# Banded attention and two mixer blocks in one kernel: a weight's split halves issued ahead of the exponentials, early row scaling on one engine, two masks built on GpSimd

## The chip, the core and the metric

The kernel runs on one core of a Trainium2 chip. The metric is the device time of one launch in microseconds (us), the median of several runs; less is better. Five engines run their own instruction queues in order and wait for one another by semaphores: TensorE (PE; the loading of its weights is listed as PEld), VectorE (DVE), ScalarE (ACT), GpSimd (POOL) and SyncE (SP), which here only starts transfers.

## The reference, cut to what matters

```
attention, batch 2, 8 heads, 768 positions, head size 64:
  s = (q @ k^T) / 8
  keep = (key < n_sink) | (0 <= query - key < window)      # n_sink 4, window 128
  a = softmax(where(keep, s, -1e9));  x = a @ v            # [2, 768, 512]
mixer 1:  h = relu(x @ w_in);  u, v = halves of h
          v_n = layernorm(v);  gated = u * (w_spatial @ v_n + b);  x = gated @ w_out
mixer 2:  u = x + token MLP(x);  out = u + channel MLP(u)
```

All matrices of the mixers are multiplied as high and low halves: a product takes three matmuls, high by high, low by high, high by low. So every weight must be split into a high part (a rounding copy) and a low part (the weight less its high part) before it is used. The weights `w_in` and others arrive as 64-bit floats, whose words VectorE first shifts and merges into 32-bit floats.

## The kernel before, in words

**Stages.** The attention comes first; the first matrix of mixer 1 (`w_in`) is worked beside it, in pieces called fills, since TensorE has time to spare there. The rest of the mixers follows and depends on TensorE nearly alone.

**Steps of the attention.** A block is 128 queries (12 blocks `j`: 6 for each of 2 batches); a step `n` (from -3 on, 24 of them with all parts) is half a block, 4 heads. The loop of `banded` (L339) is a software pipeline written out by hand: in step `n` it issues, in this order, the reciprocal of the row sums of step n+1 (`sums`, DVE L184 and L185), the transposes of step n's weights (PE L253) and their copies out of PSUM (`a_out`: ACT L261; and for a block that has a left neighbour DVE `aL`, L264), the scaling of step n+1 (`norm`), the score matmuls of step n+3 (PE L177), their masking and row maximum (`scores`: DVE L202 and L207), the exponentials of step n+2 (`expo`: ACT L223, 4 of them), and in even steps the difference of two blocks of v (`v_step`: POOL `dv`, L271). Then come the preparation of a weight (`pump`), the product with v of step n-1 (PE `pv`, L287), every second step the result of a block (`x_out`: ACT `xTH` L315, DVE `xTL` L316) and fills. Each engine's queue has its instructions in the order of issue; nothing reorders them.

**The product with v has one accumulator.** `pv` of a new block can only start when `xTL` of the block before has been read out of it (DVE L316).

**Weights.** In steps -1 to 6 (`PUMPS`) one 128x512 piece of `w_in` is prepared in each: three DVE instructions merge the words into `wi` (L464, L468, L471). Its halves are issued by `flush` one step later, from `pump`: the high part on ACT (L482) and the low part on POOL (L483). The last one has a `flush` of its own in step 7 (L366).

**Scaling.** `norm` multiplies the 4 heads' exponentials by their reciprocals: heads 0 and 1 by an ACT instruction each (L238), heads 2 and 3 by one POOL instruction (L234); the few sink columns of all 4 by another POOL instruction (`eS`, L242).

**Masks.** `masks` (L89) builds three masks on DVE before the first `scores`. m0 is needed first (step -3 and -2), m1 in step -1, m2 from step 1 on.

Of the kernel before, what the change touches and what calls it, by code (L numbers as in the profile page):

```python
# [12 lines left out]
ALU = mybir.AluOpType  # L13
PSUM = bass.MemoryType.PSUM

P = 128
# [8 lines left out]
SK = 16  # L25
# [4 lines left out]

LQ, LE, LN = 3, 2, 1
PUMPS = range(-1, 7)
BUDGET = 1900


# [4 lines left out]
class Kernel:  # L40
# [48 lines left out]
    def masks(self, pool):  # L89
        nc = self.nc  # L90
        V = nc.vector
        ta, tb = (pool.tile([P, 4, P], F32, name=x, tag=x, bufs=2) for x in ("aT", "aL"))
        rel, pos, kD, kP, kS, t = *(ta[:, x] for x in range(4)), tb[:, 0], tb[:, 1]
        nc.gpsimd.iota(rel, pattern=[[-1, P]], base=0, channel_multiplier=1, allow_small_or_imprecise_dtypes=True)
        nc.gpsimd.iota(pos, pattern=[[1, P]], base=0, channel_multiplier=0, allow_small_or_imprecise_dtypes=True)

        self.low = pool.tile([P, P], F32, name="low")
        self.up = pool.tile([P, P], F32, name="up")
        self.lowT = pool.tile([P, P], F32, name="lowT")
        V.tensor_scalar(out=self.low, in0=rel, scalar1=0.0, scalar2=None, op0=ALU.is_ge)  # L100
        V.tensor_scalar(out=self.up, in0=rel, scalar1=0.0, scalar2=None, op0=ALU.is_lt)
        V.tensor_scalar(out=self.lowT, in0=rel, scalar1=0.0, scalar2=None, op0=ALU.is_le)
        self.scalars(self.cp)
        m0 = pool.tile([P, P], F32, name="m0")
        m1 = pool.tile([P, KW], F32, name="m1")
        m2 = pool.tile([P, KW], F32, name="m2")

        def put(dst, keep):
            V.tensor_scalar(out=dst, in0=keep, scalar1=NEG, scalar2=-NEG, op0=ALU.mult, op1=ALU.add)

        V.tensor_scalar(out=kD, in0=rel, scalar1=self.win, scalar2=None, op0=ALU.is_lt)
        V.scalar_tensor_tensor(out=kD, in0=rel, scalar=0.0, in1=kD, op0=ALU.is_ge, op1=ALU.mult)
        V.tensor_scalar(out=kS, in0=pos, scalar1=self.ns, scalar2=None, op0=ALU.is_lt)

        V.tensor_tensor(out=t, in0=kD, in1=kS, op=ALU.max)
        put(m0, t)

        V.tensor_scalar(out=kP, in0=rel, scalar1=float(P), scalar2=self.win, op0=ALU.add, op1=ALU.is_lt)
        V.tensor_tensor(out=t, in0=kD, in1=kP, op=ALU.max)
        put(m1[:, 0:P], t)  # L120
        put(m2[:, 0:P], t)
        put(m2[:, P:KW], kS[:, 0:SK])

        V.tensor_tensor(out=t[:, 0:SK], in0=kS[:, 0:SK], in1=kP[:, 0:SK], op=ALU.is_gt)
        put(m1[:, P:KW], t[:, 0:SK])
        self.msk = [m0, m1, m2, m2, m2, m2]

# [100 lines left out]
    def norm(self, g):  # L228

        nc = self.nc  # L230
        j, ph = divmod(g, 2)
        r = self.rs[g]
        e = self.e[j][:, 4 * ph : 4 * ph + 4]
        nc.gpsimd.tensor_tensor(  # L234
            out=e[:, 2:4, 0:P], in0=e[:, 2:4, 0:P], in1=r[:, 2:4].unsqueeze(2).to_broadcast([P, 2, P]), op=ALU.mult
        )
        for c in range(2):
            nc.scalar.activation(out=e[:, c, 0:P], in_=e[:, c, 0:P], func=AF.Copy, scale=r[:, c : c + 1])  # L238
        if j % NB:
            if ph == 0:  # L240
                self.eS[j] = self.ap.tile([P, H, SK], F32, name="eS", tag="eS", bufs=2)
            nc.gpsimd.tensor_tensor(  # L242
                out=self.eS[j][:, 4 * ph : 4 * ph + 4], in0=e[:, :, P:KW],
                in1=r.unsqueeze(2).to_broadcast([P, 4, SK]), op=ALU.mult,
            )
# [79 lines left out]
    def banded(self):  # L325
        self.q, self.vb, self.vsb, self.ps_s, self.ss, self.e, self.sm, self.rs = {}, {}, {}, {}, {}, {}, {}, {}
        self.aT, self.ps_x, self.aS, self.dv, self.eS = {}, {}, {}, {}, {}
        NJ = B * NB
        self.kr = self.ap.tile([P, NC4, RING, KW], F32, name="kr")
        self.vf = self.ap, "vf", 2  # L330
        self.scalar_loads(self.cp)
        self.load_qk(0, 2)
        self.warm(10)
        self.load_qk(1)
        self.prefetch()
        self.load_v(0)
        self.load_qk(2)
        self.masks(self.ap)
        for n in range(-LQ, NG + 2):  # L339
            j, ph = divmod(n, 2)  # L340
            self.xdone = self.xnext
            if ph and n >= -1:
                if (n + 7) // 2 < NJ:
                    self.load_qk((n + 7) // 2)
                if (n + 3) // 2 < NJ:
                    self.load_v((n + 3) // 2)
            if 0 <= n + LN < NG:
                self.sums(n + LN)
            if 0 <= n < NG:
                self.a_transpose(n)  # L350
                self.a_out(n)
            if 0 <= n + LN < NG:
                self.norm(n + LN)
            if n + LQ < NG:
                self.qk(n + LQ)
                if n < 0:
                    self.warm(3)
                self.scores(n + LQ)
            if 0 <= n + LE < NG:
                self.expo(n + LE)  # L360
            if 0 <= n < NG and ph == 0 and j % NB:
                self.v_step(j)
            self.step()
            if n in PUMPS:
                self.pump()
            if n == max(PUMPS) + 1:  # L366
                self.flush()
            if 0 <= n - 1 < NG:
                self.pv(n - 1)
                if ph == 0:  # L370
                    if (j - 1) % NB:
                        self.sinks_mm(j - 1)

                    self.fill_until(j - 1)
                    self.x_out(j - 1)
            if 0 <= n < NG and ph == 1 and j % NB:
                self.sinks(j)
            if n == NG - 4:
                self.raws = [self.spatial_load(r) for r in range(2)]
            self.fill(BUDGET)  # L380
        self.xdone = self.xnext
        self.vf = self.sp, "tmp", 4
# [541 lines left out]
```

## Time and profile before

| | |
|---|---|
| median of 3 runs | 499.09 us (498.95 to 500.24) |
| the profiled execution | 499.52 us, its span 497.7 us |
| busy: PE, DVE, ACT, POOL | 95%, 56%, 35%, 29% of the span |
| mean granted TensorE clock | 0.978 of 2.4 GHz |
| PE in 40 slices | `8589799999999999999999899999999999999994` |
| DVE in 40 slices | `6989864675553489946979798765222211311112` |
| granted clock in 40 slices | `9859899999999999999999999999999999999998` |

One slice is 12.4 us. A digit is the busy share in tenths, or the granted clock in tenths. The share of the whole span says little here: the first five slices are another program than the rest, as the digits of PE and DVE show. Everything that the change touches runs in the first 75 us.

### The profile page before, as it was taken

What the parts mean: (1) busy time and instruction counts of PE and PEld (TensorE: products, weight loads), DVE (VectorE), ACT (ScalarE), POOL (GpSimd) and SP (SyncE); (2) the same over time, 40 slices, a digit from 0 to 9 for tenths busy, and PEclk for the clock granted to TensorE, in tenths of its full rate; (3) what the DMA queues carried; (4) which work ended last, traced back from release to release, by engine and by line L of the source; (5) the groups of instructions that cost most, each with busy time, mean ns of one, the idle gap of its engine ahead of it and who ended that gap; (6) DMA issues with size and microseconds to landing.
All of it is one profiled execution on the core that took longest, in us unless ns stands there. A gap on an engine that the chain in (4) does not pass through costs nothing.

```text
span 497.7 us, 7141 instructions
## 1 busy us (share of the span) xinstructions
PE 473.5 (95%) x2672; PEld 395.4 (79%) x2672; DVE 280.5 (56%) x631; ACT 176.5 (35%) x471; POOL 145.3 (29%) x164
## 2 busy tenths in 40 slices
PE   8589799999999999999999899999999999999994
PEld 7357588788888999998888578888888888888883
DVE  6989864675553489946979798765222211311112
ACT  4556677686754322235542222222101110011000
POOL 1453742354344557652543133222100000000000
PEclk9859899999999999999999999999999999999998
DMA  8844131402005022313544244221020000200002
GB/s 265 264 149 139 65 97 38 153 23 86 2 2 211 1 84 65 96 32 105 170 127 131 83 126 128 84 86 42 2 84 0 1 0 1 85 1 0 0 1 91
DMA packets 19788, 38.82 MB, mean 78 GB/s; under 512 B 1825, under 2 KB 8225, under 8 KB 19745
## 3 DMA queue, kind: packets, MB, share of 16 engines
q1 hardware_dynamic: 19312, 38.02, 24.1%
q8 instruction: 23, 0.38, 0.3%
q10 hardware_dynamic: 432, 0.26, 0.2%
q14 instruction: 21, 0.16, 0.1%
HBM read 35.13 MB, written 3.15 MB: 77 GB/s over the span
## 4 chain that ended last, share of the span: by engine, by line
PE 82%; DVE 13%; ACT 1%; issue 1%; DMA 1%; POOL 0%; POOLq 0%; ACTq 0%
PE pso L59 7%; PE pso L57 7%; PE pso L58 7%; PE psc L57 6%; PE psc L59 6%; PE psc L58 6%; PE pv L287 4%; PE psg L59 3%; PE psg L58 3%; PE psg L57 3%; PE sc L177 3%; DVE wi L468 2%; PE psu L57 2%; PE ps L59 2%; PE ps L57 2%; PE ps L58 2%
## 5 line engine op out<-in xcount | busy, mean ns | idle before, releaser
L630 DVE SCALAR_TENSOR_TENSOR hh<-psc,hh 128x512 fp32r<-128x512 f32 x36 | 24.9, 692 | 127.9 <-ACT hh L629 127.8
L629 ACT ACTIVATE hh<-psc 128x512 fp32r<-128x512 f32 x36 | 21.5, 597 | 157.1 <-PE psc L59 157.1
L59 PE MATMUL pso<-c2H,hh 128*128 128x512 f32 x144 | 56.3, 391 | 1.2 <-DVE hh L630 1.2
L57 PE MATMUL pso<-c2H,hh 128*128 128x512 f32 x144 | 56.8, 394 | 0.0
L58 PE MATMUL pso<-c2L,hh 128*128 128x512 f32 x144 | 56.1, 390 | 0.0
L471 DVE SCALAR_TENSOR_TENSOR wi<-rawi,wi 128x512 int32<-128x512 int32 (+2 forms) x46 | 41.2, 895 | 1.6
L223 ACT ACTIVATE e<-s,nm 128x144 f32<-128x144 f32 (+1 forms) x96 | 38.1, 399 | 4.0 <-DVE nm L207 4.0
L468 DVE SCALAR_TENSOR_TENSOR wi<-rawi,wi 128x512 int32<-128x512 int32 (+2 forms) x46 | 36.4, 791 | 1.6
L464 DVE TENSOR_SCALAR wi<-rawi 128x512 int32<-128x512 int32 (+2 forms) x46 | 32.8, 712 | 0.7 <-POOL c1L L483 0.6
L59 PEld LDWEIGHTS pso<-c2H,hh 128*128 128x128 f32 x144 | 27.0, 188 | 7.3 <-DVE hh L630 1.6
L57 PE MATMUL psg<-wsTH,vnH 128*128 128x384 f32 x96 | 32.1, 334 | 0.0
L58 PE MATMUL psg<-wsTL,vnH 128*128 128x384 f32 x96 | 32.1, 334 | 0.0
L59 PE MATMUL psg<-wsTH,vnL 128*128 128x384 f32 x96 | 32.1, 334 | 0.0
L58 PEld LDWEIGHTS pso<-c2L,hh 128*128 128x128 f32 x144 | 27.1, 188 | 5.4
L57 PEld LDWEIGHTS pso<-c2H,hh 128*128 128x128 f32 x144 | 27.1, 188 | 5.4
L177 PE MATMUL sc<-kr,q 64*128 64x272 f32 (+2 forms) x192 | 29.5, 424 | 1.1 <-DVE nm L207 0.7
L59 PE MATMUL psc<-u2H,c 128*128 128x512 f32 x72 | 28.0, 389 | 0.0
L57 PE MATMUL psc<-u2H,c1H 128*128 128x512 f32 x72 | 28.0, 389 | 0.0
L58 PE MATMUL psc<-u2L,c1H 128*128 128x512 f32 x72 | 28.0, 389 | 0.0
L59 PE MATMUL psc<-u2H,c1L 128*128 128x512 f32 x72 | 28.0, 389 | 0.0
L57 PE MATMUL psc<-u2H,c 128*128 128x512 f32 x72 | 28.0, 389 | 0.0
L58 PE MATMUL psc<-u2L,c 128*128 128x512 f32 x72 | 28.0, 389 | 0.0
(139 smaller groups left out, 1108.7 us busy)
## 6 DMA issues: line engine op xcount, KB each, us to landing
rawi<-in_moe_w_ch SPq DMA_DIRECT2D x24, 512.0 KB, 3.6
rawi<-in_moe_w_in SPq DMA_DIRECT2D x8, 512.0 KB, 4.7
kr<-in_k SPq DMA_DIRECT2D x11, 288.0 KB, 4.2
v<-in_v SPq DMA_DIRECT2D x12, 256.0 KB, 3.8
out_x<-o SPq DMA_DIRECT2D x12, 256.0 KB, 2.3
q<-in_q SPq DMA_DIRECT2D x11, 256.0 KB, 4.9
raws<-in_w_spT SPq DMA_DIRECT2D x6, 384.0 KB, 3.9
rawi<-in_moe_w_out SPq DMA_DIRECT2D x4, 512.0 KB, 5.0
```

Of the source, the lines that this page charges most:

```text
L57: self.nc.tensor.matmul(ps, lh, rh, start=(first and i == 0), stop=False)
L58: self.nc.tensor.matmul(ps, lh, rl, start=False, stop=False)
L59: self.nc.tensor.matmul(ps, ll, rh, start=False, stop=(last and i == n - 1))
L177: nc.tensor.matmul(o, q[r, p, :], k, start=True, stop=True)
L223: nc.scalar.activation(out=self.e[j][:, 4 * ph + c, :u], in_=s[:, c, :u], func=AF.Exp, bias=nm[:, c : c + 1], scale=-1.0, accum_out=sm[:, ...
L287: nc.tensor.matmul(ps[h * D : (h + 1) * D, p, :], w[:, (2 * p + h) * D : (2 * p + h + 1) * D], self.aT[g][c][:, 2 * x + h, :], start=(p == ...
L464: V.tensor_scalar(out=wi, in0=hi, scalar1=3, scalar2=0x3FFFFFFF, op0=ALU.logical_shift_left, op1=ALU.bitwise_and,)
L468: V.scalar_tensor_tensor(out=wi, in0=hi, scalar=-0x40000000, in1=wi, op0=ALU.bitwise_and, op1=ALU.bitwise_or)
L471: V.scalar_tensor_tensor(out=wi, in0=lo, scalar=29, in1=wi, op0=ALU.logical_shift_right, op1=ALU.bitwise_or)
L629: nc.scalar.activation(out=h, in_=ps, func=AF.Relu)
L630: nc.vector.scalar_tensor_tensor(out=l, in0=ps, scalar=0.0, in1=f32(h), op0=ALU.max, op1=ALU.subtract)
```

## The change

Three edits. `flush` is now called in every step right behind `norm`, so a weight's high part stands on ACT ahead of the step's exponentials and its low part on POOL ahead of `dv`. `norm` scales all 4 heads on ACT for the first 11 half blocks (`NORMA`), and POOL's instruction for heads 2 and 3 is issued only from there on. In `masks`, everything after m0 is issued to GpSimd instead of VectorE; two operations are written in other terms, one of them as two instructions.

```
+NORMA = 11
...
         V.tensor_tensor(out=t, in0=kD, in1=kS, op=ALU.max)
         put(m0, t)
 
+        V = nc.gpsimd
         V.tensor_scalar(out=kP, in0=rel, scalar1=float(P), scalar2=self.win, op0=ALU.add, op1=ALU.is_lt)
-        V.tensor_tensor(out=t, in0=kD, in1=kP, op=ALU.max)
+        V.tensor_tensor(out=t, in0=kD, in1=kP, op=ALU.add)
         put(m1[:, 0:P], t)
         put(m2[:, 0:P], t)
         put(m2[:, P:KW], kS[:, 0:SK])
 
-        V.tensor_tensor(out=t[:, 0:SK], in0=kS[:, 0:SK], in1=kP[:, 0:SK], op=ALU.is_gt)
+        V.tensor_tensor(out=t[:, 0:SK], in0=kS[:, 0:SK], in1=kP[:, 0:SK], op=ALU.mult)
+        V.tensor_tensor(out=t[:, 0:SK], in0=kS[:, 0:SK], in1=t[:, 0:SK], op=ALU.subtract)
         put(m1[:, P:KW], t[:, 0:SK])
...
-        nc.gpsimd.tensor_tensor(
-            out=e[:, 2:4, 0:P], in0=e[:, 2:4, 0:P], in1=r[:, 2:4].unsqueeze(2).to_broadcast([P, 2, P]), op=ALU.mult
-        )
-        for c in range(2):
+        if g >= NORMA:
+            nc.gpsimd.tensor_tensor(
+                out=e[:, 2:4, 0:P], in0=e[:, 2:4, 0:P], in1=r[:, 2:4].unsqueeze(2).to_broadcast([P, 2, P]), op=ALU.mult
+            )
+        for c in range(2 if g >= NORMA else 4):
             nc.scalar.activation(out=e[:, c, 0:P], in_=e[:, c, 0:P], func=AF.Copy, scale=r[:, c : c + 1])
...
             if 0 <= n + LN < NG:
                 self.norm(n + LN)
+            self.flush()
             if n + LQ < NG:
...
             if n in PUMPS:
                 self.pump()
-            if n == max(PUMPS) + 1:
-                self.flush()
```

On POOL, the queue of steps 1, 2 and 3 of the kernel before (`e`: scaled exponentials, `eS`: sink columns, `wvL`: a weight's low part, `dv`: the difference of v blocks):

```order
L234 TENSOR_TENSOR e_259<-e_259,r_278 128x2x128
L242 TENSOR_TENSOR eS_291<-e_259,r_278 128x64
L483 TENSOR_TENSOR wvL_77<-wi_267,wvH_76 128x512
L234 TENSOR_TENSOR e_259<-e_259,r_325 128x2x128
L242 TENSOR_TENSOR eS_291<-e_259,r_325 128x64
L271 TENSOR_TENSOR dv_361<-v_195,v_120 128x512
L483 TENSOR_TENSOR wvL_77<-wi_314,wvH_76 128x512
L234 TENSOR_TENSOR e_355<-e_355,r_382 128x2x128
L242 TENSOR_TENSOR eS_397<-e_355,r_382 128x64
L483 TENSOR_TENSOR wvL_77<-wi_365,wvH_76 128x512
```

The same steps on POOL in the changed kernel:

```order
L246 TENSOR_TENSOR eS_295<-e_264,r_281 128x64
L486 TENSOR_TENSOR wvL_77<-wi_272,wvH_76 128x512
L246 TENSOR_TENSOR eS_295<-e_264,r_329 128x64
L486 TENSOR_TENSOR wvL_77<-wi_320,wvH_76 128x512
L275 TENSOR_TENSOR dv_368<-v_196,v_120 128x512
L246 TENSOR_TENSOR eS_403<-e_362,r_387 128x64
L486 TENSOR_TENSOR wvL_77<-wi_372,wvH_76 128x512
```

The scaling of two heads is gone, and in the even step `dv` stands behind the low part, where it stood ahead of it.

On ACT, steps 1 and 2 of the kernel before (`wvH`: a weight's high part; the rows of L223 are the exponentials, `xTH` a block's result):

```order
L261 ACTIVATE aT_286<-tr_281 128x512
L238 ACTIVATE e_259<-e_259,r_278 128x128 x2
L223 ACTIVATE e_259,sums_307<-s_251,nm_252 128x144 x4
L482 ACTIVATE wvH_76<-wi_267 128x512
L261 ACTIVATE aT_333<-tr_328 128x512
L238 ACTIVATE e_259<-e_259,r_325 128x128 x2
L223 ACTIVATE e_355,sums_356<-s_299,nm_300 128x144 x4
L482 ACTIVATE wvH_76<-wi_314 128x512
L315 ACTIVATE xTH_74<-pv_320 128x4x128
```

The same steps on ACT in the changed kernel:

```order
L265 ACTIVATE aT_289<-tr_284 128x512
L242 ACTIVATE e_264<-e_264,r_281 128x128 x4
L485 ACTIVATE wvH_76<-wi_272 128x512
L226 ACTIVATE e_264,sums_313<-s_256,nm_257 128x144 x4
L265 ACTIVATE aT_337<-tr_332 128x512
L242 ACTIVATE e_264<-e_264,r_329 128x128 x4
L485 ACTIVATE wvH_76<-wi_320 128x512
L226 ACTIVATE e_362,sums_363<-s_305,nm_306 128x144 x4
L319 ACTIVATE xTH_74<-pv_324 128x4x128
```

Four scalings instead of two, then the high part, then the exponentials. The queues of PE and SP hold the same instructions in the same order; DVE's lacks seven mask instructions and is otherwise the same.

## Rows read from the trace of the kernel before

**Rows 1.** Windows: stretch, its length, busy us (count) of each engine, clock, DMA.
```profile
0.00:55.86 55.86, 42.63 (x296) 30.65 (x297) 48.42 (x166) 32.17 (x112) 24.27 (x36) 0.88 0.61 196
55.86:150.00 94.14, 93.53 (x791) 77.15 (x792) 57.19 (x221) 63.84 (x213) 40.65 (x64) 0.98 0.17 54
```

**Rows 2.** Timeline, step 1: start, length, engine, line, out<-in [idle before <-releaser].
```profile
18.96 0.18 DVE L185 RECIPROCAL r<-r 128x4 f32<-128x4 f32 x1
...
19.24 0.69 ACT L238 ACTIVATE e<-e,r 128x128 f32<-128x128 f32 x2 [1.69 <-DVE r L185]
19.84 0.40 ACT L223 ACTIVATE e<-s,nm 128x144 f32<-128x144 f32 x1
...
20.88 0.42 DVE L464 TENSOR_SCALAR wi<-rawi 128x512 int32<-128x512 int32 x1
...
21.43 0.62 ACT L482 ACTIVATE wvH<-wi 128x512 fp32r<-128x512 f32 x1
...
22.13 1.76 POOL L483 TENSOR_TENSOR wvL<-wi,wvH 128x512 fp32r<-128x512 f32 x1 [2.04 <-ACT wvH L482]
...
22.68 1.23 DVE L184 TENSOR_SCALAR r<-sums 128x4 f32<-128x4 f32 x1
```

**Rows 3.** Timeline of POOL and DVE, step 2.
```profile
25.02 1.27 POOL L271 TENSOR_TENSOR dv<-v 128x512 f32<-128x512 f32 x1
...
26.45 0.42 DVE L464 TENSOR_SCALAR wi<-rawi 128x512 int32<-128x512 int32 x1
...
27.63 1.63 DVE L471 SCALAR_TENSOR_TENSOR wi<-rawi,wi 128x512 int32<-128x512 int32 x1
29.19 0.68 DVE L316 TENSOR_TENSOR xTL<-pv,xTH 128x512 fp32r<-128x512 f32 x1
```

**Rows 4.** Timeline of POOL and DVE much later, a low part and L464 meeting.
```profile
257.44 1.31 POOL L483 TENSOR_TENSOR c1L<-wi,c1H 128x512 fp32r<-128x512 f32 x1 [1.76 <-ACT c1H L482]
...
257.49 1.54 DVE L464 TENSOR_SCALAR wi<-rawi 128x512 int32<-128x512 int32 x1
```

**Rows 5.** Timeline of POOL and DVE, end of step 6.
```profile
53.04 1.61 POOL L534 TENSOR_TENSOR vnL<-vf,vnH 128x512 fp32r<-128x512 f32 x1 [0.81 <-ACT vnH L533]
53.57 1.64 DVE L471 SCALAR_TENSOR_TENSOR wi<-rawi,wi 128x512 int32<-128x512 int32 x1
54.62 1.72 POOL L483 TENSOR_TENSOR wuL<-wi,wuH 128x512 fp32r<-128x512 f32 x1
```

**Rows 6.** Timeline of ACT and DVE, step 4.
```profile
37.02 0.68 ACT L238 ACTIVATE e<-e,r 128x128 f32<-128x128 f32 x2
37.16 0.69 DVE L264 TENSOR_TENSOR aL<-tr,lowT 128x512 f32<-128x512 f32 x1 [1.53 <-ACT aT L261]
...
39.60 0.42 DVE L464 TENSOR_SCALAR wi<-rawi 128x512 int32<-128x512 int32 x1
40.06 1.68 DVE L468 SCALAR_TENSOR_TENSOR wi<-rawi,wi 128x512 int32<-128x512 int32 x1
```

**Rows 7.** Timeline of DVE and PE, end of step 6.
```profile
55.13 0.68 DVE L316 TENSOR_TENSOR xTL<-pv,xTH 128x512 fp32r<-128x512 f32 x1
...
55.86 0.44 PE L287 MATMUL pv<-aT,v 128*64 128x128 f32 x4 [2.52 <-DVE xTL L316]
```

**Rows 8.** Windows, the stretch of step 7.
```profile
56.54:61.96 5.42, 5.42 (x30) 4.18 (x28) 3.37 (x17) 3.60 (x14) 3.72 (x8) 0.71 0.01 5
```

**Rows 9.** Timeline of PE, step 9.
```profile
70.23 0.44 PE L57 MATMUL psu<-xTH,wuH 128*128 128x384 f32 x1 [0.57 <-ACT aS L298]
```

**Rows 10.** Timeline of PE and DVE, the first scores.
```profile
5.66 0.71 PE L177 MATMUL sc<-kr,q 64*128 64x128 f32 x8
...
7.11 0.28 DVE L207 CUSTOM_DVE_ANT_0 s<-sc,m 128x128 f32<-128x128 f32 x1
...
7.66 0.92 PE L177 MATMUL sc<-kr,q 64*128 64x128 f32 x8 [0.42 <-DVE nm L207]
...
8.20 0.29 DVE L207 CUSTOM_DVE_ANT_0 s<-sc,m 128x128 f32<-128x128 f32 x1 [0.17 <-PE sc L177]
```

## The prediction

> **What bounds the kernel now.** I read the windows by stage first, then the timeline of each engine over the first 80 us, then who waits for whom. Two stages stand apart [rows 1]: up to 55.86 us DVE is busy for 48.42 of 55.86 us and PE for 42.63; from there to 150 us PE is busy for 93.53 of 94.14 us. So until about 56 us the time is set by DVE's queue, and behind that by TensorE, whose work is the same in both kernels. The hinge between the stages is the read-out of block 2: PE's `pv` waits 2.52 us for DVE's `xTL` and starts at 55.86 [rows 7]. From there PE hardly pauses, so a microsecond by which that `xTL` moves should move the end by a microsecond. The sum below is the shift of that `xTL`, and of one wait behind it.
>
> The reader should also see what DVE loses. L184, a 128x4 instruction, takes 1.23 us while POOL writes a low part from 22.13 on [rows 2], where its other instances take 0.16; L471 takes 1.63 or 1.64 [rows 3, 5], L468 1.68 [rows 6], where they take 0.69 undisturbed. Each weight's low part costs DVE one such hold of 0.94 to 1.07 us: POOL's subtraction and a DVE instruction that works on SBUF alone exclude each other. Not so with `dv` at 25.02 [rows 3], which runs beside the mask additions that read PSUM: none of them is longer there.
>
> **Where the low part lands now.** Take the start of L185 as zero of a step. ACT's first scaling starts at 0.28 (19.24 less 18.96), two scalings take 0.60 (to 19.84), the low part starts 0.70 after the high part (21.43 to 22.13) [rows 2]. With four scalings the high part starts at 0.28 + 1.20 = 1.48 and the low part at 2.18; it lasts 1.3, so to 3.48. DVE's first weight instruction, L464, starts at 1.92 in a step without `aL` (20.88 less 18.96) [rows 2] and 2.54 behind L184's end in a step with it (26.45 less 23.91) [rows 2, 3], 2.51 in this count. So the low part moves ahead by about a microsecond, but not far enough: it still meets the weight instructions.
>
> Steps 0 and 1 (no `aL`): it arrives during L464, and L468 is held as at 40.06: 1.68 less 0.69, +0.99 [rows 6]. In place of this the hold of L184 goes, 1.23 less 0.16 = 1.07. Change -0.08 each, -0.16.
>
> Step 2: the low part holds the pair when L464 comes. At 257.49 L464 in that place ended 0.28 behind POOL's end [rows 4]; so it would end at 3.76 instead of 2.93, +0.83. Now `dv` is queued behind the low part, not ahead of it. After POOL's instruction the waiting DVE instruction goes first, then POOL's next one: `vnL`, L471 and `wuL` took turns so [rows 5]. So `dv` goes behind L464, and holds L468: +0.99. Together 1.82 against the 0.94 of L471 before (1.63 less 0.69) [rows 3]: +0.88.
>
> Step 3: its holds end under a wait. `aL` at 37.16 had idled 1.53 us for a chain through PE that starts from step 2's `xTL` at 29.19 [rows 3, 6]; that chain passes the shift on, no more.
>
> Step 4: scaling starts with the copy of PE's transposes, at 37.02 [rows 6]; high part 38.22, low part 38.92 to 40.22. L464 at 39.60 would end at 40.50 instead of 40.02, +0.48; `dv` then holds L468, +0.99. Before: 0.99 [rows 6]. Change +0.48.
>
> Step 5 has one hold before and one after: 0.
>
> Step 6: low part 0.83 and `dv` 0.99 as in step 2; and `vnL`, whose high part ACT does behind the exponentials, is now third on POOL and takes its turn before L471, +0.95 (1.64 less 0.69) [rows 5]. Together 2.77 against 0.95 before, where `wuL` at 54.62 ran beside instructions that read PSUM: +1.82.
>
> **ACT.** Exponentials end at 0.28 + 1.20 + 0.62 + 1.59 = 3.69 in this count (21.43 less 19.84 for four) [rows 2], and the next L184 needs them at 3.72 (22.68) at the earliest, 4.7 with a hold: the cover is thin, but I cost it at nothing; without a hold it would be the next bound. Behind 56 us two scalings more, 0.60 us, lie under PE's fills except in step 9, where PE waits for ACT's `aS` already [rows 9] and `aS` stands behind scalings and exponentials: +0.6 there (0 if PE's own queue is later by then).
>
> **Masks.** Seven instructions leave DVE ahead of its first mask addition at 7.11. It could not start before 6.20: the scores start at 5.66, and 0.54 passes from such a start to DVE's taking them (7.66 to 8.20) [rows 10]. So at most -0.91. POOL's two first mask instructions fall beside DVE's two-input ones that make m0, and exclude them; the trace has no mask on POOL, and by the holds above each could cost DVE some 0.3, so -0.2 at least. I take -0.6. The rest of POOL's masks is done before m1 is read. The Trainium skill (Perfetto Trace Analysis, Optimizing Scalar/DVE Operations) says that the two engines share a read port, so that moving work between them may not help; taken at its word this term is 0 and the time 0.6 longer.
>
> **Sum.** -0.6 - 0.16 + 0.88 + 0.48 + 1.82 = +2.42 at the `xTL` of step 6, +0.6 in step 9: +3.0, which I shade to +2.9 as the last wait may be smaller. The profiled execution, 499.52 us, would become 502.4; it lies 0.43 above the median of 499.09, so the forecast is 502.0 for the median.
>
> **Rivals.**
>
> Clock. PE's pause before 55.86 grows from 2.5 us to nearly 5, that before block 2's `pv` by some 0.6. In the 5.42 us behind the first the granted clock is 0.71 [rows 8], so 2 x 0.29 x 5.42 = 3.1 us at 1.2 instead of 2.4 GHz, which cost half, 1.6 us. If the longer pauses bring one more such spell: 503.6. For it: such pauses are where the clock fell. Against: a pause that is only longer has the fall inside it, which costs nothing.
>
> DVE keeps its turn, so not slower. If DVE's three weight instructions, issued on one another's heels, go before POOL's waiting `dv` and `vnL`, these run under `xTL`, which reads PSUM. Steps 2 and 4 then cost 0.99 less each and step 6 1.94 less: 3.9 less, +2.9 becomes -1.0: 498.1, and 497.2 with the whole 0.91 from the masks and the half of step 9's wait. It decides at the moment when L464 ends in steps 2, 4 and 6. Against it: POOL got in between L468 and L471 in [rows 5]. The Trainium skill (SBUF — State Buffer, Who interferes with whom) says that issue order, not the kind of operation, decides who blocks; `dv` is issued ahead of L468, so by that rule this rival falls, and the rows so far agree.
>
> Holds gone, so faster. If the low part lands wholly under the mask additions, DVE loses none of 1.07 + 1.07 + 0.94 + 0.99 + 0.95 = 5.0 us, and with 0.6 from the masks the time is 493.5. It needs the low part a good microsecond earlier than 2.18, that is scalings that don't wait for L185. Only that DVE might be later than I reckon speaks for it.
>
> **How the numbers follow.** Forecast 0.57 (its own range 501.1 to 503.4, from the masks' bounds, step 9 and a little clock); clock 0.13; DVE keeps its turn 0.21; holds gone 0.09. Within 0.3% (1.5 us, about what a measurement of this kernel tells from no change) is most of the third case and the low edge of the first: 0.22. Faster is the fourth case and the low part of the third and small things: 0.20. Slower: 0.58. The range of 8 in 10 takes in the third case and the clock, not the fourth: 497.0 to 504.4.
>
> **What would show it.** Right: in steps 0 and 1 L184 at 0.16 and L468 at 1.7; in steps 2, 4 and 6 L464 about 1.2 to 1.5 and L468 1.7, with `dv` between them; L471 1.6 in step 6; `pv` of block 3 near 58 us; PE's wait for `aS` in step 9 near 1.2 us. The first mask addition near 6.5 us. Wrong: weight instructions of 0.42 and 0.69 in the even steps, or `pv` of block 3 starting at or before 55.9 us.

## The result, and the profile after

The changed kernel takes 502.28 us (median of 7 runs, 502.19 to 503.27), the kernel before 499.49 us (7 runs, 498.95 to 501.25): a ratio of 1.0057 with a 95% interval from 1.0039 to 1.0076, so 2.8 us slower. The forecast was 502.0 us, by a mechanism that it priced at +2.9. The profiled execution took 503.15 us, with a span of 501.4 at a granted clock of 0.975; that of before took 499.52, span 497.7, clock 0.978.

In the new numbering, L187 and L188 stand for L184 and L185, L467, L471 and L474 for the weight instructions L464, L468 and L471, L485 and L486 for a weight's high and low part (L482, L483), L268 for `aL`, L275 for `dv`, L533 for the scaling of `vf` (L530), L537 for `vnL`, L320 for `xTL`, L210 for the mask additions (L207). The masks' instructions on GpSimd end early and don't return below.

Who PE waited for, in the whole span (us in total, times, longest); first of the kernel before:

```profile
PE pv L287 <- DVE xTL L316: 5.6, 3, 2.5
PE psu L57 <- ACT aS L298: 0.6, 1, 0.6
```

and of the kernel after:

```profile
PE pv L291 <- DVE xTL L320: 8.5, 3, 4.2
PE psu L58 <- ACT aS L302: 1.2, 1, 1.2
```

The 2.9 us more are in the first of the two, the wait for the read-out by DVE, and most of that in its longest instance, at the hinge of block 2. PE's own rows show that instance and the one wait behind it, after (start, length, engine, line, out<-in, [idle before <-releaser]):

```profile
57.69 0.70 PE L291 MATMUL pv<-aT,v 128*64 128x128 f32 x4 [4.25 <-DVE xTL L320]
...
73.57 0.44 PE L58 MATMUL psu<-xTH,wuH 128*128 128x384 f32 x1 [1.15 <-ACT aS L302]
```

`pv` starts 1.83 us later than at 55.86 [rows 7], and the `psu` of step 9 3.34 us later than at 70.23 [rows 9].

DVE after, from the first mask addition to the read-out of block 2, in steps -3, -2, 1, 2, 4, 5 and 6:

```profile
6.18 0.29 DVE L210 CUSTOM_DVE_ANT_0 s<-sc,m 128x128 f32<-128x128 f32 x1 [0.18 <-PE sc L180]
...
7.69 0.29 DVE L210 CUSTOM_DVE_ANT_0 s<-sc,m 128x128 f32<-128x128 f32 x1 [0.58 <-PE sc L180]
...
20.16 0.42 DVE L467 TENSOR_SCALAR wi<-rawi 128x512 int32<-128x512 int32 x1
20.62 1.67 DVE L471 SCALAR_TENSOR_TENSOR wi<-rawi,wi 128x512 int32<-128x512 int32 x1
22.33 0.69 DVE L474 SCALAR_TENSOR_TENSOR wi<-rawi,wi 128x512 int32<-128x512 int32 x1
22.94 0.16 DVE L187 TENSOR_SCALAR r<-sums 128x4 f32<-128x4 f32 x1
...
25.64 1.21 DVE L467 TENSOR_SCALAR wi<-rawi 128x512 int32<-128x512 int32 x1
26.88 1.63 DVE L471 SCALAR_TENSOR_TENSOR wi<-rawi,wi 128x512 int32<-128x512 int32 x1
28.55 0.69 DVE L474 SCALAR_TENSOR_TENSOR wi<-rawi,wi 128x512 int32<-128x512 int32 x1
29.16 0.68 DVE L320 TENSOR_TENSOR xTL<-pv,xTH 128x512 fp32r<-128x512 f32 x1
...
39.57 0.86 DVE L467 TENSOR_SCALAR wi<-rawi 128x512 int32<-128x512 int32 x1
40.47 1.65 DVE L471 SCALAR_TENSOR_TENSOR wi<-rawi,wi 128x512 int32<-128x512 int32 x1
...
42.76 0.68 DVE L320 TENSOR_TENSOR xTL<-pv,xTH 128x512 fp32r<-128x512 f32 x1
...
46.85 1.22 DVE L533 TENSOR_SCALAR vf<-vf,st 128x512 f32<-128x512 f32 x1
...
52.48 1.21 DVE L467 TENSOR_SCALAR wi<-rawi 128x512 int32<-128x512 int32 x1
53.72 1.64 DVE L471 SCALAR_TENSOR_TENSOR wi<-rawi,wi 128x512 int32<-128x512 int32 x1
55.39 1.64 DVE L474 SCALAR_TENSOR_TENSOR wi<-rawi,wi 128x512 int32<-128x512 int32 x1
56.95 0.68 DVE L320 TENSOR_TENSOR xTL<-pv,xTH 128x512 fp32r<-128x512 f32 x1
```

And POOL after, in steps 1, 2 and 6:

```profile
20.39 1.35 POOL L486 TENSOR_TENSOR wvL<-wi,wvH 128x512 fp32r<-128x512 f32 x1 [1.54 <-ACT wvH L485]
...
25.28 1.29 POOL L486 TENSOR_TENSOR wvL<-wi,wvH 128x512 fp32r<-128x512 f32 x1 [1.53 <-ACT wvH L485]
26.52 1.45 POOL L275 TENSOR_TENSOR dv<-v 128x512 f32<-128x512 f32 x1
...
52.12 1.28 POOL L486 TENSOR_TENSOR wuL<-wi,wuH 128x512 fp32r<-128x512 f32 x1 [1.54 <-DMA q<-in_q]
53.37 1.44 POOL L275 TENSOR_TENSOR dv<-v 128x512 f32<-128x512 f32 x1
54.77 1.70 POOL L537 TENSOR_TENSOR vnL<-vf,vnH 128x512 fp32r<-128x512 f32 x1
```

The two lists are to be read against each other. In step 2, L467 is taken up at 25.64, while the low part runs from 25.28, and ends 0.28 after it; `dv`, queued behind the low part, comes next and L471 waits for it; by L474 POOL's queue is empty and 0.69 is back. In step 6 three POOL instructions in a row cost three DVE instructions in a row 0.79, 0.95 and 0.95 us. Before, steps 2 and 6 had one held instruction each [rows 3, 5].

Behind the hinge the granted clock differs as well. Windows of the same length (stretch, length, busy us and count of PE, PEld, DVE, ACT, POOL, clock, DMA), first before:

```profile
55.86:62.00 6.14, 6.14 (x36) 4.88 (x38) 4.06 (x19) 3.64 (x14) 4.24 (x9) 0.72 0.01 4
```

then after:

```profile
57.69:63.83 6.14, 6.14 (x30) 4.97 (x30) 4.75 (x18) 3.55 (x14) 3.41 (x6) 0.56 0.02 4
```

At 0.72, 2 x 0.28 x 6.14 = 3.4 us of the stretch are at 1.2 GHz; at 0.56, 5.4 us. The 2.0 us more at half speed cost about 1.0 us of PE's work. What made the spell longer stays open. In the run with the masks alone (below), `pv` of block 3 had waited 2.52 us, as before, and yet the clock behind it is lower still:

```profile
54.40 0.69 PE L290 MATMUL pv<-aT,v 128*64 128x128 f32 x4 [2.52 <-DVE xTL L319]
```
```profile
54.40:60.54 6.14, 6.14 (x28) 4.89 (x29) 4.01 (x18) 2.97 (x12) 4.25 (x9) 0.52 0.02 5
```

### The profile page after: what moved, and what is told of

The parts are those of the page before. It is cut to its first block, busy times and chain, and to the rows that moved or that the text cites. A ratio compares the mean times of both kernels' runs of the same rounds, so it can differ in the third digit from the quotient of the medians.

```text
span 501.4 us, 7160 instructions
## 1 busy us (share of the span) xinstructions
PE 474.8 (95%) x2672; PEld 396.3 (79%) x2672; DVE 282.1 (56%) x624; ACT 182.4 (36%) x493; POOL 139.7 (28%) x161
## 4 chain that ended last, share of the span: by engine, by line
PE 83%; DVE 13%; ACT 2%; issue 1%; POOL 0%; POOLq 0%; DVEq 0%; ACTq 0%
PE pso L60 7%; PE pso L58 7%; PE pso L59 6%; PE psc L60 6%; PE psc L58 6%; PE psc L59 6%; PE pv L291 4%; PE psg L59 3%; PE psg L58 3%; PE psg L60 3%; DVE wi L471 3%; PE sc L180 3%; PE psu L58 2%; PE ps L59 2%; PE ps L58 2%; PE ps L60 2%
## 5 line engine op out<-in xcount | busy, mean ns | idle before, releaser
L474 DVE SCALAR_TENSOR_TENSOR wi<-rawi,wi 128x512 int32<-128x512 int32 (+2 forms) x46 | 39.3, 853 | 1.6
L471 DVE SCALAR_TENSOR_TENSOR wi<-rawi,wi 128x512 int32<-128x512 int32 (+2 forms) x46 | 39.2, 852 | 1.6
L467 DVE TENSOR_SCALAR wi<-rawi 128x512 int32<-128x512 int32 (+2 forms) x46 | 35.6, 773 | 0.6 <-POOL c1L L486 0.6
L242 ACT ACTIVATE e<-e,r 128x128 f32<-128x128 f32 x70 | 23.0, 391 | 16.4 <-DVE r L188 16.4
L291 PE MATMUL pv<-aT,v 128*64 128x128 f32 x192 | 20.7, 304 | 8.5 <-DVE xTL L320 8.5
L60 PE MATMUL psc<-u2H,c 128*128 128x512 f32 x72 | 28.0, 389 | 0.0
```

The costliest lines, as they stand in the source:

```text
L60: self.nc.tensor.matmul(ps, ll, rh, start=False, stop=(last and i == n - 1))
L291: nc.tensor.matmul(ps[h * D : (h + 1) * D, p, :], w[:, (2 * p + h) * D : (2 * p + h + 1) * D], self.aT[g][c][:, 2 * x + h, :], start=(p == ...
L467: V.tensor_scalar(out=wi, in0=hi, scalar1=3, scalar2=0x3FFFFFFF, op0=ALU.logical_shift_left, op1=ALU.bitwise_and,)
L471: V.scalar_tensor_tensor(out=wi, in0=hi, scalar=-0x40000000, in1=wi, op0=ALU.bitwise_and, op1=ALU.bitwise_or)
L474: V.scalar_tensor_tensor(out=wi, in0=lo, scalar=29, in1=wi, op0=ALU.logical_shift_right, op1=ALU.bitwise_or)
```

## The experiments

Theory A says that the loss is DVE's, by exclusion: what counts is which instructions of DVE each GpSimd instruction meets, and moving either past the other brings the time back. Theory B says that it is ACT's: scalings and high parts now stand ahead of the exponentials there, and PE and DVE wait for those. The first three runs do one part of the change alone, the others mend it. Each was run 6 to 12 times, beside the kernel before: the first four on one chip, where its median was 500.44 us, the others on a second, where it was 499.2. The ratios come from all the runs and are not the quotients of the medians. The expected times count from 499.5 us for the kernel before, so they are held against the ratios as shares of that.

### The early flush alone

```diff
             if 0 <= n + LN < NG:
                 self.norm(n + LN)
+            self.flush()
...
-            if n == max(PUMPS) + 1:
-                self.flush()
```

> The kernel before with one edit: the halves of a weight are issued behind the scaling and ahead of the exponentials; scaling stays half on ACT, half on GpSimd, masks stay on VectorE. Theory A (VectorE and GpSimd exclude each other, and what counts is where each GpSimd instruction meets VectorE's three weight instructions): with two scalings on ACT the low part starts 1.58 us behind L185, so it holds L464 for about 0.8 in steps 0 and 1 (before: 1.07 each on L184), for about 0.2 in steps 2 and 6, where the difference of v blocks, now behind it, then holds L468 for 0.99, and the layer norm's low part holds L471 for 0.95 in step 6. Sum: -0.5 +0.3 +0 +1.2 and -0.7 from step 5, near +0.3: 499.3 to 500.5. Theory B (the load on ACT ahead of the exponentials is what costs): the high part ahead of the exponentials delays them by 0.5 us in each of 8 steps; as half of the load that the change adds, half of its loss, +1.4: 500.9.

Measured: 499.49 us, ratio 0.9994 [0.9978, 1.001]. No difference that can be told: A's range, 0.9996 to 1.002, overlaps the interval, and B's figure, 1.0028, lies above it. With two scalings ahead of it the low part comes earlier, so L463 (the first weight instruction) takes the hold of L184 in steps 0 and 1; L184 stands at 0.16. DVE in step 0:

```profile
15.90 1.22 DVE L463 TENSOR_SCALAR wi<-rawi 128x512 int32<-128x512 int32 x1
17.15 0.69 DVE L467 SCALAR_TENSOR_TENSOR wi<-rawi,wi 128x512 int32<-128x512 int32 x1
```

The hold has moved from L184 to L463, and it costs 0.8 instead of 1.07. In steps 2 and 6 `dv` holds L467 (1.64 in both), as A had it.

### The scaling on ScalarE alone

```diff
+NORMA = 11
...
+        if g >= NORMA:
             nc.gpsimd.tensor_tensor(... e[:, 2:4, 0:P] ...)
-        for c in range(2):
+        for c in range(2 if g >= NORMA else 4):
```

> The kernel before with one edit: the first 11 half blocks are scaled by ACT alone; the halves of a weight stay behind the exponentials, masks stay on VectorE. Theory A: the high part comes 0.6 us later, so the low part starts 3.77 us behind L185 instead of 3.17, when VectorE's weight instructions are over or in their last one; the holds of 1.07, 1.07, 0.94, 0.99 and 0.95 us go, or fall on instructions off the path; against that +0.6 from the wait for aS in step 9. Faster, by 2 to 4.4: 495 to 497.5. Theory B: two scalings more on ACT in each of 11 steps, so slower than before by about half of the change's loss or more: 500.5 to 502.

Measured: 497.34 us, ratio 0.9947 [0.9929, 0.9965]. ACT has the same work here as in the changed kernel, and the kernel is faster than before by 2.6 us: B falls, and A's range, 0.991 to 0.996, holds the ratio. With the flush still behind the exponentials, the two scalings more push the low part of steps 0 and 1 past the weight instructions altogether. DVE, step 1:

```profile
20.23 0.42 DVE L466 TENSOR_SCALAR wi<-rawi 128x512 int32<-128x512 int32 x1
20.69 0.69 DVE L470 SCALAR_TENSOR_TENSOR wi<-rawi,wi 128x512 int32<-128x512 int32 x1
21.41 0.69 DVE L473 SCALAR_TENSOR_TENSOR wi<-rawi,wi 128x512 int32<-128x512 int32 x1
22.02 0.16 DVE L185 TENSOR_SCALAR r<-sums 128x4 f32<-128x4 f32 x1
22.22 0.18 DVE L186 RECIPROCAL r<-r 128x4 f32<-128x4 f32 x1
```

and POOL there, whose low part starts 0.03 after L185:

```profile
22.05 1.28 POOL L485 TENSOR_TENSOR wvL<-wi,wvH 128x512 fp32r<-128x512 f32 x1 [2.37 <-ACT wvH L484]
```

The expectation had the holds of the steps with `aL` gone as well, or off the path. Only that of step 6 went: the last weight instruction, L473, still takes 1.67, 1.66 and 1.67 us in steps 2, 4 and 5, as the low part arrives just ahead of it there.

### The masks alone

```diff
+        V = nc.gpsimd
-        V.tensor_tensor(out=t, in0=kD, in1=kP, op=ALU.max)
+        V.tensor_tensor(out=t, in0=kD, in1=kP, op=ALU.add)
...
-        V.tensor_tensor(out=t[:, 0:SK], ..., op=ALU.is_gt)
+        V.tensor_tensor(out=t[:, 0:SK], in0=kS[:, 0:SK], in1=kP[:, 0:SK], op=ALU.mult)
+        V.tensor_tensor(out=t[:, 0:SK], in0=kS[:, 0:SK], in1=t[:, 0:SK], op=ALU.subtract)
```

> The kernel before with one edit: the second and third mask on GpSimd. Both theories: the first mask addition comes 0.9 us earlier, and by the changed kernel's trace 0.3 of it is lost again to a wait for score matmuls, so -0.6: 498.9. In the changed kernel's sum the same -0.6 is used.

Measured: 500.03 us, ratio 0.9999 [0.9982, 1.0016]. The -0.6 expected is inside the interval, and so is nothing: inconclusive at this size. In the trace L187 of step -1 starts at 8.82 instead of 9.11, which is -0.29 and half of what was expected; PE's first scores start 0.26 us later in this execution (5.92 for 5.66).

### The changed kernel with `dv` issued ahead of the flush

```diff
+            if 0 <= n < NG and ph == 0 and j % NB:
+                self.v_step(j)
             self.flush()
...
-            if 0 <= n < NG and ph == 0 and j % NB:
-                self.v_step(j)
```

> The changed kernel with the difference of v blocks issued ahead of a weight's halves in even steps, as it stood before; nothing else differs. Theory A: dv runs beside the mask additions again, which read PSUM and aren't held, and L468 falls back from 1.65 to 0.69 us in steps 2, 4 and 6; 2.9 us less on VectorE's path, and the pause of TensorE ahead of block 3 shorter, so perhaps its low clock too: 499.4, at the lowest 498.5. Theory B: ACT has the same work in the same order, so no change: 502.3.

Measured: 499.02 us, ratio 0.999 [0.9974, 1.0006]; A's two figures are 0.9998 and 0.998, B's is 1.0056, and the changed kernel's interval began at 1.0039. Scalings, exponentials and flush are as in the changed kernel; `dv` alone changes its place, and the loss is gone. That is theory A's case, and it is also the one test of the order on POOL by itself. POOL in step 2:

```profile
24.25 1.27 POOL L275 TENSOR_TENSOR dv<-v 128x512 f32<-128x512 f32 x1
25.83 1.28 POOL L486 TENSOR_TENSOR wvL<-wi,wvH 128x512 fp32r<-128x512 f32 x1 [0.30 <-ACT wvH L485]
```

and DVE:

```profile
26.18 1.21 DVE L467 TENSOR_SCALAR wi<-rawi 128x512 int32<-128x512 int32 x1
27.43 0.69 DVE L471 SCALAR_TENSOR_TENSOR wi<-rawi,wi 128x512 int32<-128x512 int32 x1
28.16 0.69 DVE L474 SCALAR_TENSOR_TENSOR wi<-rawi,wi 128x512 int32<-128x512 int32 x1
```

`dv` runs under the mask additions, which read PSUM, and holds nothing: L471 is at 0.69 in steps 2, 4 and 6. The low parts hold as before, and `vnL` still holds L474 in step 6 (1.64).

The Trainium skill (SBUF — State Buffer, Who interferes with whom) has issue order decide who blocks. The two kernels, which differ in that order alone, agree with it: 1.63 us for L471 with `dv` issued just ahead of it, 0.69 with `dv` issued earlier.

### The changed kernel with the flush ahead of the scalings

```diff
+            self.flush()
             if 0 <= n + LN < NG:
                 self.norm(n + LN)
-            self.flush()
```

> The changed kernel with a weight's halves issued ahead of the scaling instead of behind it; all else as in the changed kernel. Theory A: the high part starts when the step begins, so the low part runs from about 0.6 to 1.9 us behind L185, beside the transposed copy and the mask additions that read PSUM, and holds nothing: L464 0.42, L468 and L471 0.69 in steps 0, 1, 3 and 5. In even steps the difference of v blocks follows the sink columns, 2.2 to 3.5 us, and holds L464 for about 0.8; the layer norm's low part still holds L471 in step 6. Sum against the changed kernel -1.0 -1.0 -1.0 -0.5 -0.7 -0.9 = -5: 497.2. Theory B (load on ACT): same load in another order, the scaling 0.14 us later: no faster than 502.

Measured: 496.79 us, ratio 0.9942 [0.992, 0.9964]; A's figure, 497.2, is 0.9954. The low part of step 2 now starts at 22.89, 0.8 behind L187 instead of 2.3, and ends before the weight instructions come; those of steps 0, 1, 3 and 5 are free (one L467 at 0.53). What is left is `vnL`, which holds L474 in step 6 (1.64), and `dv`, here at 24.38, which meets L467 in the even steps:

```profile
24.78 1.16 DVE L467 TENSOR_SCALAR wi<-rawi 128x512 int32<-128x512 int32 x1
25.97 0.69 DVE L471 SCALAR_TENSOR_TENSOR wi<-rawi,wi 128x512 int32<-128x512 int32 x1
26.70 0.69 DVE L474 SCALAR_TENSOR_TENSOR wi<-rawi,wi 128x512 int32<-128x512 int32 x1
```

### Step 9's wait: scaling on ScalarE up to one block less

```diff
-NORMA = 11
+NORMA = 10
```

> The changed kernel with the first 10 half blocks scaled by ACT alone instead of 11, so that step 9 has two scalings less on ACT and GpSimd's instruction again. If the sink copy aS of step 9 stands behind those scalings on the path, TensorE's wait for it falls from 1.15 to 0.57 us and the time by 0.6: 501.7. If TensorE would be late there anyway: no change.

Measured: 501.35 us, ratio 1.0045 [1.0025, 1.0065], against 1.0057 [1.0039, 1.0076] for the changed kernel. The wait for `aS` goes back to that of before:

```profile
72.72 0.44 PE L58 MATMUL psu<-xTH,wuH 128*128 128x384 f32 x1 [0.56 <-ACT aS L302]
```

So the wait was the two scalings' doing, 0.59 us by the trace; the times alone, whose intervals overlap, don't show it.

### The changed kernel without the early flush

From the kernel just shown, the early `self.flush()` is taken out and the one behind the exponentials put back.

> The changed kernel without the early issue of a weight's halves (they stand behind the exponentials as before), and with 10 half blocks scaled by ACT alone. Theory A: as the kernel with the scaling alone changed, which measured 0.9947 of the kernel before, less 0.6 for step 9 and up to 0.6 for the masks: ratio near 0.993, so the early issue is the whole of the loss. Steps 0 and 1 show L464 0.42, L468 and L471 0.69, L184 0.16. Theory B, that the parts add up: parts of 0.9994, 0.9947 and 0.9999 give 0.994 for all three, which the changed kernel's 1.0057 already contradicts.

Measured: 496.61 us, ratio 0.9947 [0.9928, 0.9966]. Against 1.0045 of the run before, on the same chip, this prices the early flush where it stands, behind four scalings: 0.98%, 4.9 us. Steps 0 and 1 are free of holds, as A had it. A's 0.993 lies at the lower end of the interval; a gain over the scaling alone, from step 9 and the masks, is not seen in the ratios.

### Flush and `dv` ahead of the scalings

Meant to beat both kernels: flush and `v_step` moved ahead of `norm`, `NORMA = 10`.

> A version meant to beat both: masks on GpSimd, 10 half blocks scaled by ACT alone, a weight's halves ahead of the scaling, and in even steps the difference of v blocks right behind them, ahead of the sink columns. Theory A: the low part runs 0.6 to 1.9 us behind L185 and holds nothing, the difference of v blocks 1.9 to 3.1 us, so that L464 of even steps is held for some 0.4; only the layer norm's low part in step 6 still costs 0.95. Against the kernel before -1.07 -1.07 -0.5 -0.6 -0.96 and 0.4 for step 6, some -3.8 with the masks: 0.992. It also may meet a new bound: without holds the exponentials end at 3.8 us, just behind VectorE's 3.7.

Measured: 496.89 us, ratio 0.9936 [0.9911, 0.9962]: faster than before and after, but not told apart from the two before it in this list that gained. L467 of the even steps falls to 0.92, 0.95 and 0.94; only step 6 keeps a full hold, for `vnL`. The bound that A named, the exponentials, is not met: from step 0 to the `xTL` of step 6 DVE's one wait is that of step 4 for the transposed weights (2.54 us).

### All kernels side by side

For each kernel, this adds up by how much L187, the three weight instructions and the scaling of `vf` (here by after's names) exceed their shortest time (0.16; 0.42, 0.69, 0.69; 0.54) in the timeline up to the `xTL` of step 6:

| kernel | DVE held, us | ratio to before |
|---|---|---|
| after | 9.25 | 1.0057 |
| scaling up to one block less | 9.24 | 1.0045 |
| masks alone | 6.99 | 0.9999 |
| before | 6.96 | 1 |
| `dv` ahead of the flush | 6.40 | 0.999 |
| early flush alone | 6.36 | 0.9994 |
| scaling alone | 4.04 | 0.9947 |
| no early flush | 4.02 | 0.9947 |
| flush ahead of the scalings | 3.34 | 0.9942 |
| flush and `dv` ahead | 2.61 | 0.9936 |

The order by held time is the order by ratio, but for two pairs of neighbours a few hundredths of a microsecond apart. (The hold of step 3, some 0.8 to 1.1 us in most of them, lies under a wait for PE and is counted all the same.) From the last row to the first, 6.64 us of holds go with 0.0121 x 499.5 = 6.0 us. The ratios hold some clock as well: 34 of the 58 runs of before had a mean granted clock of 0.979 or less, none of the 12 with the scaling alone; whether the edits themselves raise it is not shown. Among the single runs whose granted clock was 0.981 or more, over all the runs on record, the kernel before took 499.0 us (median of 24), the changed kernel 502.3 (3), the one with the scaling alone 497.3 (12), the one with the flush ahead of the scalings 496.6 (9), the one with `dv` ahead too 496.9 (6). So at like clock the loss is 3.3 us, and these gains are 1.7 to 2.4 us, where the ratios give 2.6 to 3.2. The parts don't add: alone they give -0.06%, -0.53% and -0.01%, together +0.57%.

## Why the prediction was right

Point by point, as the prediction had it:

- **What bounds the kernel.** Right: the loss is built up before the hinge and appears as PE's wait for `xTL`, 4.25 instead of 2.52 us.
- **Masks, -0.6.** Right in this execution: L187 of step -1 starts at 8.54 instead of 9.11, -0.57; with the masks alone it was -0.29. The first mask addition gained 0.93 (7.11 to 6.18), but the next pick-up then waits 0.58 us for PE's scores, so the gain is bounded by PE. The mask instructions on GpSimd hardly held DVE: two of its own beside them took 0.35 and 0.39 us instead of 0.29 and 0.28. The Trainium skill (Perfetto Trace Analysis, Optimizing Scalar/DVE Operations) doubts such an offload; the run with the masks alone, at 0.9999, can't decide between the two.
- **Steps 0 and 1.** Right: L187 at 0.16, L471 at 1.66 and 1.67, so +0.97 and +0.98 for -1.07, where the sum had +0.99.
- **Step 2, +0.88.** Right in kind, L467 and L471 held and `dv` between them, with L467 at 1.21 where 1.25 was expected. The `xTL` stands at 29.16 instead of 29.19 where the sum came to +0.12.
- **Step 3, nothing.** Right: from the `xTL` of step 2 to the `aL` of step 4 it takes 7.97 us in both.
- **Step 4, +0.48.** Right in kind (L467 0.86, where the sum had 0.90 and the signs 1.2 to 1.5; L471 1.65); its `xTL` comes 0.38 later than before where the sum had 0.60.
- **Step 5, 0.** Mis-sized: -0.27. The low part now holds the scaling of `vf` (1.22) and leaves the weight instructions free; from the `xTL` of step 4 to L187 of step 6 the time falls by about that.
- **Step 6, +1.82.** From L187 to `xTL` it takes 7.17 us instead of 5.45, +1.72. Three holds, as predicted.
- **ACT, nothing.** Right up to the hinge: from step 0 on DVE's only wait there is the one of step 4 for the transposed weights, 1.70 us (1.53 before).
- **The sum at the hinge.** +2.42 was predicted and +1.82 measured (55.13 to 56.95). Up to the `xTL` of step 2 the terms were too high by 0.15 together, those of steps 4, 5 and 6 by 0.07, 0.27 and 0.10.
- **Step 9, +0.6.** The wait for `aS` went from 0.57 to 1.15, +0.58, and the smaller scaling range took it back.

The span grew by 3.7 in the profiled executions and the medians by 2.8. The sum at the hinge and step 9 together gave +2.4 where +3.0 was predicted; the rest of the shift of 3.34 us at step 9 is the clock, about 1.0 us by the two windows. So what the clock rival described, which the sum had at nothing, is part of this execution: a longer spell at 1.2 GHz behind the pause. That the longer pause brought it is not shown, since the masks alone had no shorter one behind a pause of 2.52 us. As far as this execution stands for the others, the forecast of 502.0 meets the median of 502.28 so closely by some luck, through two errors of opposite sign. The loss is not the clock's alone: in single runs at 0.981 or more the two kernels take 502.3 and 499.0 us, at 0.979 or less 502.9 and 500.8 (medians of 3, 24, 4 and 34 runs). How the 2.8 us between the medians divide stays open: no run here changes the clock alone.

One statement of the prediction is wider than the traces: that POOL's subtraction and a DVE instruction that works on SBUF alone exclude each other. It holds for the instructions that the sum uses, but not for every one. Before, in step 6, the statistics of `vf` are not held beside `wuL`, which runs from 54.62 to 56.34 [rows 5]; they take the 0.68 us that they also take at 42.98, where POOL is idle:

```profile
55.73 0.68 DVE L525 BATCH_NORM_STATS2 st<-vf 128x6 f32<-128x512 f32 x1
```

And in the run with the scaling alone, L186, a reciprocal in SBUF, takes its usual 0.18 us beside the low part at 22.05.

**The rivals.** DVE does not keep its turn: L471 and L474 waited for `dv` and `vnL`, which stood in POOL's queue while DVE was still held. (That rival's lower figure, 497.2, does not add up: 0.31 and 0.3 us off 498.1 give 497.5.) The holds did not go, but they could: the two kernels with the flush ahead of the scalings, where the low part lands almost wholly beside PSUM reads, show what that rival described, at 0.9942 and 0.9936 (496.6 and 496.3 from 499.5), where it gave 493.5. Its size was too large: it left out its own +0.6 of step 9, and in the better of them `dv` and `vnL` still hold DVE for most of the 2.61 us that are left.

## What to carry to other kernels

When two engines exclude each other, an instruction on the one has no price of its own: it costs what it happens to meet, so write for each step when the one queue issues and what the other engine does at that moment, and put the excluded work beside reads of PSUM. Edits that each shift such an instruction don't add; one that gains alone (0.9947) can lose (1.0045) with a second that is neutral alone (0.9994). Before moving a producer earlier, look at what waits in line behind its consumer, for here `dv`, which the change had not touched, took up the whole loss: one place earlier in POOL's queue it gave all of it back (0.999).

## What was not expected of the hardware

Runs of one and the same kernel differ by some 1.8 us, along with the mean granted clock: of the kernel before, 29 of the 34 runs at 0.971 to 0.979 took 500.1 to 502.0 us, the 24 at 0.981 to 0.988 all from 498.3 to 499.7. The profiled executions show such a spell behind the read-out of block 0, where the work is nearly the same in all. Windows, of before, after, and `dv` ahead of the flush in turn:

```profile
29.00:37.00 8.00, 7.08 (x36) 5.58 (x38) 6.42 (x20) 3.44 (x13) 3.81 (x6) 0.57 0.28 81
```
```profile
29.00:37.00 8.00, 7.10 (x36) 5.61 (x38) 6.22 (x20) 4.05 (x16) 1.88 (x3) 0.58 0.26 87
```
```profile
29.00:37.00 8.00, 7.50 (x57) 5.82 (x59) 7.21 (x24) 5.61 (x20) 3.11 (x4) 0.79 0.39 121
```

At a clock of 0.57 PE has 36 instructions on record there, at 0.79 it has 57. From the `xTL` of step 2 to the `aL` of step 4 it takes 7.97 us in the first two and 6.81 in the third (28.77 to 35.58). So a start time read from two single executions can differ by about a microsecond for this alone, as much as a term of the sum. Behind the hinge it is more: from the `xTL` of step 6 to the end of the span the ten profiled executions take 442.5 to 445.2 us, before 442.6, after 444.5, the masks alone 444.9, and the order is not that of the holds. So a microsecond at the hinge is not seen as a microsecond in the span of one execution; the ratios of many runs are what the verdicts above rest on.
